# One transformer kernel on Trainium2: the product of w_out and w_gate with w_gate stationary in four column tiles

## The chip, the cores and the metric

The kernel runs on one core of one Trainium2 chip. The metric is the device time of one execution in microseconds, and what is compared is the median of the executions shown. All rows come from one profiled execution of the program. Its engines are TensorE (PE, with its weight loads listed apart as PEld), VectorE (DVE), ScalarE (ACT), GpSimd (POOL) and SyncE (SP), which here only starts transfers.

## What is computed

The reference is attention with a soft cap, followed by a gated product and by a layer of eight experts of which each token uses one:

```python
scores = cap * np.tanh(scale * (q @ k.T) / cap)      # 4 x 12 heads, 448 x 64
attn = softmax(scores); x = attn @ v                 # x: 1792 x 768
x2 = ((x @ w1) * (x @ w2)) @ w3 @ w_out              # 768 -> 1024 -> 1024 -> 768
logits = x2 @ w_gate + modality_bias[modality_id]    # 768 -> 8
e = argmax(logits);  g = softmax(logits)[e]
out = g * (relu(x2 @ moe2_w1[e]) @ moe2_w2[e])
```

The kernel multiplies the weights first: it makes w3 @ w_out once, and it appends to w_out the eight columns of w_out @ w_gate, so that the logits come out of the same products as x2. The product w_out @ w_gate (1024 x 768 by 768 x 8) is what the change touches.

## The kernel before

The first stage, about the first third of the time, does three things interleaved: attention for 24 pairs of heads; the narrowing of the weights, which arrive as 64-bit words and are turned into 32-bit floats by integer operations on VectorE; and the fold, w3 @ w_out, in 32 halves. The order is written by a list planner, `Schedule` (line 20). Each piece of work is a task with an engine (or a choice of two), an estimated duration in ns, a key, the tasks that it depends on, and the buffers that it takes and frees. The planner always emits the task that can start first by its estimates; the engines then run the emitted order, each strictly in its own queue. TensorE tasks also have a mode, "full" for the whole array and "tiles" for 64x64 tiles: the planner charges 190 ns for a change of mode (line 32) and prefers work of the mode that it is in (line 84).

w_out comes in eight chunks of 128 rows. For each chunk c (lines 780 to 815): one load, the narrowing of the chunk into a buffer `y`, two times three transposes by TensorE into a bank of PSUM (`tr_wo`, line 578), each evicted by ScalarE or VectorE (`wo_copy`, line 586) into the tile `woT`; then the gate product (`wo_gate`, line 589), six products that add up over the 768 rows of w_gate; and then `wo_split` (line 594), two VectorE instructions that write the eight columns, as a rounded high part and a low part, beside the chunk's own. The first eight fold pairs need the splits of chunks 0 to 3, the last eight those of chunks 4 to 7. The next chunk's transposes wait for the gate before (`gate[-1:]`, line 797).

The gate, the transposes of k, q, w_out and w3, all take their PSUM bank from one pool of two, "tr" (`bank("tr", 2)`). The 64x64 products of attention (scores line 487, pv line 507, sums line 534) use other banks, `sc` and `pv`.

In the gate before, `lhsT`, the operand that is loaded into the array, is a 128x128 block of w_out transposed, and `rhs`, the one that streams, is 128x8 of w_gate:

```python
for d in range(KD):     # KD = 6
    mm(wo_p[c][:, 0:NE], lhsT=wo_t[c][:, d, :], rhs=wgs[:, d, :], start=(d == 0), stop=(d == KD - 1))
```

The later stages, from about 315 us on, are the large products of the gated layer and of the experts, in an order written in the code; nothing of them is edited.

Of the kernel before, what the change touches and what calls it, by code (L numbers as in the profile page):

```python
# [8 lines left out]
F32 = mybir.dt.float32  # L9
# [5 lines left out]
ALU = mybir.AluOpType  # L15
# [105 lines left out]
def attention_moe_moe_kernel(  # L121
# [37 lines left out]
    nc = tc.nc  # L159
# [3 lines left out]
    NE = w_gate.shape[1]  # L163
    P = 128
    CP = 112
    NC = S // CP
    KD = DM // P
# [32 lines left out]
    at1 = tc.alloc_tile_pool(name="at1", bufs=2, side="right", reuse_waits="tile")  # L200
# [3 lines left out]
    def ctile(name, shape, dt=F32):  # L204
        return cp.tile(shape, dt, name=name, tag=name)

    mm = nc.tensor.matmul
# [3 lines left out]
    ident = ctile("ident", [P, P])  # L211
# [38 lines left out]
    def cast(out_, in_, eng):  # L250
        if eng is nc.scalar:
            nc.scalar.copy(out_, in_)  # L252
        else:
            eng.tensor_copy(out_, in_)
# [8 lines left out]
    class Stream:  # L263
# [17 lines left out]
        def add(self, pieces):  # L281
            n = len(pieces)
            self.todo += [(p, i, n) for i, p in enumerate(pieces)]
# [123 lines left out]
    def bank(tag, bufs):  # L407
        return psa.tile([P, 512], F32, name=tag, tag=tag, bufs=bufs)
# [55 lines left out]
    ENG = {"ACT": nc.scalar, "DVE": nc.vector, "POOL": nc.gpsimd}  # L464
# [71 lines left out]
    def sum_out(p, eng):  # L536
        smt[p] = at1.tile([P, 2, S], F32, name="smt", tag="smt", bufs=2)
        cast(smt[p], smb[p][:, :, :S], ENG[eng])
# [30 lines left out]
    w3raw, w3r = {}, {}  # L569


    wgs = at1.tile([P, KD, NE], F32, name="wgs", tag="wgs", bufs=1)
    wo_y, wo_u, wo_t, wo_p = {}, {}, {}, {}

    def load_wg():
        nc.sync.dma_start(wgs, w_gate.rearrange("(a p) e -> p a e", p=P))

    def tr_wo(c, j):
        if j == 0:
# [6 lines left out]
    def wo_copy(c, j, eng):  # L586
        cast(wo_t[c][:, 3 * j:3 * j + 3, :], wo_p[c, j][:, 0:3 * P].rearrange("p (a f) -> p a f", a=3), ENG[eng])

    def wo_gate(c):
        wo_p[c] = bank("tr", 2)  # L590
        for d in range(KD):
            mm(wo_p[c][:, 0:NE], lhsT=wo_t[c][:, d, :], rhs=wgs[:, d, :], start=(d == 0), stop=(d == KD - 1))

    def wo_split(c):
        g = wo_p[c][:, 0:NE].rearrange("p (a h c) -> p a h c", a=1, h=2)
# [6 lines left out]
    w3p, w3t, fos, sts = {}, {}, {}, {}  # L602
# [126 lines left out]
    def leave_at2():  # L729
# [7 lines left out]
    NW = 14  # L737
    sch = Schedule({
        "raw": 2, "tr": 2, "KT": 3, "QT": 3, "v": NV, "sc": 2, "th": 7, "th3": 2, "sums": 2, "smt": 2, "pv": 1, "pvs": 2,
        "w3raw": 2, "w3r": 2, "w3t": 2, "wst": 2, "wraw": 2, "y": 3, "unit": 5,  # L740
    }, {"SP": 691.0, "ACT": 750.0, "DVE": 1570.0, "POOL": 2010.0, "PE": 1450.0})
    add = sch.add

    def do(fn, *args):
        return lambda: fn(*args)
# [3 lines left out]
    for c in range(30):  # L749
        add("PE", 175, 1e6, lambda: nc.tensor.transpose(warm[:, 0:P], ident, ident),  # L750
            take=[("tr", "warm")] if c == 0 else [], use=[("tr", "warm")])
# [11 lines left out]
    wg_in = add("SP", 630, -4, load_wg, dma=100)  # L763
# [5 lines left out]
    gate, augs = [], []  # L769
# [6 lines left out]
    def cast_c(c, eng):  # L776
        ws.cast1(ENG[eng], False)
        if c < 8:
            wo_u[c] = ws.part
    for c in range(NW):  # L780
        u = c // 2
        key = (4.0 * c + 3) if c < 8 else (10 + 10.0 * c)
        raw, y, un = ("wraw", c), ("y", c), ("unit", u)
        t = add("SP", 630, key - 2, ws.load1, take=[raw], use=[raw], dma=2185, deps=[ld])
        ld = t
        t = add({'ACT': (920, 600), 'DVE': (600, 0)}, 0, key, ws.abs1, [t] + ([ca] if c else []), take=[y], use=[raw, y])
        ca = t
        t = add({'DVE': (630, 0)}, 0, key, lambda eng: ws.narrow1(0, ENG[eng]), [t] + cn3[-1:], use=[raw, y])
        for i in range(1, 4):
            t = add("DVE", 630 if i == 1 else 950, key, do(narrow_c, c, i), [t], use=[raw, y])  # L790
        cn3.append(t)
        if c < 8:
            tt, tp = [("tr", "o", c, j) for j in range(2)], ("tr", "g", c)
            kg = key + 3.0
            cps = []
            for j in range(2):
                x = add("PE", 320, kg, do(tr_wo, c, j), [cn3[-1], *gate[-1:], *cps[-1:]], take=[tt[j], *([] if j else [("th", "o", c)])], use=[tt[j], y, ("th", "o", c)])
                cps.append(add({'ACT': (500, -300), 'DVE': (560, 0)}, 0, kg, lambda eng, c=c, j=j: wo_copy(c, j, eng), [x], use=[tt[j], ("th", "o", c)]))
            gate.append(add("PE", 1500, kg, do(wo_gate, c), [*cps, wg_in], take=[tp], use=[tp, ("th", "o", c)]))
        if c >= 8:  # L800
            kp = add("SP", 650, key - 5, ws.keep1, [t, cs], use=[y], dma=1092)
            t = (kp, 0)
        t = add({'ACT': (730, 0), 'DVE': (470, 600)}, 0, key, lambda eng, c=c: cast_c(c, eng), [t, cs], take=[un] if c % 2 == 0 else [], use=[y, un])

        if c < 8:
            augs.append(add("DVE", 300, key + 3.0, do(wo_split, c), [gate[c], t], use=[tp, un]))

        def sub(eng, c=c):
            ws.sub1(ENG[eng])
            if c % 2 and c < 8:  # L810
                w_outs.append(ws.take())

        cs = units[u] = add({'POOL': (1764, 0)}, 0, key, sub, [t], use=[y, un])
# [7 lines left out]
    for p in range(NP + 1):  # L821
        raw, vk, kt, qt = ("raw", p), ("v", p), ("KT", p), ("QT", p)
        hk, hq, sk, pk = ("tr", "k", p), ("tr", "q", p), ("sums", p), ("pv", p - 1)
        dep, use, take = [], [], []
        if p:
            dep, take, use = [ex[3], lv], [pk], [pk, ("th3", p - 1), ("v", p - 1)]
        if p < NP:
# [4 lines left out]
            t = add("PE", 380, 4 * p - 5.2, do(tr_k, p), [lk], take=[hk], use=[hk, raw])  # L832
            kl = add({'DVE': (620, 0), 'ACT': (530, 300)}, 0, kk, lambda eng, p=p: k_out(p, eng), [t], take=[kt], use=[hk, kt])
            t = add("PE", 380, 4 * p - 5.2, do(tr_q, p), [lq], take=[hq], use=[hq, raw])
            last_at2.append(t)
            ql = add({'DVE': (620, 0), 'ACT': (530, 300)}, 0, kk, lambda eng, p=p: q_out(p, eng), [t], take=[qt], use=[hq, qt])
            dep, take, use = dep + [kl, ql], take + [("sc", p, 3)], use + [("sc", p, 3), kt, qt]
        joint = add("PE", 770, 4 * p, do(pv_score, p), dep, take=take, use=use, mode="tiles")
        if p:

            for c in range(3):
                vl[p - 1, c] = add("PE", 770, 4 * p + c + 2.4, do(pv, p - 1, c), [ex[c], joint, vl.get((p - 1, c - 1))],
                                   use=[pk, ("th", p - 1, c), ("v", p - 1)], mode="tiles")
            smk = ("sc", "s", p - 1)
            sm = add("PE", 770, 4 * p + 2.9, do(sum_mm, p - 1), [ad], take=[smk], use=[smk, ("sums", p - 1)], mode="tiles")
            t = add({'ACT': (910, 0), 'DVE': (1090, 0)}, 0, 4 * p - 1, lambda eng, p=p: sum_out(p - 1, eng), [sm], take=[("smt", p - 1)], use=[smk, ("smt", p - 1)])
            ss = add("SP", 1260, 4 * p, do(sum_store, p - 1), [t], use=[("smt", p - 1)], dma=25)
            t = add("ACT", 530, 4 * p - 2, do(pv_copy, p - 1), [vl[p - 1, 2]], take=[("pvs", p - 1)], use=[pk, ("pvs", p - 1)])
# [4 lines left out]
            if r == H // 2 - 1 and b < B - 1:  # L853
                t = add("SP", 630, 4 * p, lambda b=b: rs_t.__setitem__(b, sums_in(b)), [ss], dma=100)
                t = add("DVE", 500, 4 * p, lambda b=b: sums_add(rs_t[b]), [t])
# [4 lines left out]
        for n, c in enumerate(ORD):  # L860
            sc, th, i = ("sc", p, c), ("th3" if c == 3 else "th", p) + (() if c == 3 else (c,)), 4 * p + n
            if c < 3:
                t = add("PE", 770, i, do(score, p, c), [joint], take=[sc], use=[sc, kt, qt], mode="tiles")
            else:
                t = joint
            t = add("ACT", 600 if c == 3 else 950, i + 0.2, do(p_tanh, p, c), [t, cap_in], take=[th], use=[sc, th])
            ex[c] = add("ACT", 580 if c == 3 else 950, i + 1.1, do(p_exp, p, c), [t], use=[th])
        for c in (1, 2, 3):
            ad = add("DVE", 660 if c == 3 else 1120, 4 * p + 0, do(psum, p, c), [ex[c], *([ex[0]] if c == 1 else []), ad],
                     take=[sk] if c == 1 else [], use=[sk, ("th3", p) if c == 3 else ("th", p, c), *([("th", p, 0)] if c == 1 else [])])  # L870


    t = add("POOL", 1000, 60, tables, [vl[15, 0]])
    t = add("SP", 4000, 60, tables_dma, [t], dma=3000)
# [6 lines left out]
    t = add("SP", 3000, 2 * NH, leave_at2, last_at2, dma=6400)  # L881
# [6 lines left out]
    t = add("SP", 1200, 2 * NH, lambda: raw0[0].append(load_rec(0, 2, xp)), raw0s[:1], dma=1274)  # L888
# [6 lines left out]
    for n, (f, g) in enumerate(SWEEP):  # L895
        key = 5.4 * (n + 2) + 3
        raw, r_, h_, w_ = ("w3raw", n), ("w3r", n), ("tr", "w", n), ("w3t", n)
        t = add("SP", 630, key - 3, do(load_w3, n), take=[raw], use=[raw], dma=1456)
        t = add({'ACT': (660, -300), 'DVE': (610, 0)}, 0, key, lambda eng, n=n: abs_w3(n, eng), [t], take=[r_], use=[raw, r_])
        t = add({'DVE': (500, 0)}, 0, key, lambda eng, n=n: conv_w3(n, 0, eng), [t], use=[raw, r_])  # L900
        for i in range(1, 4):
            t = add("DVE", (0, 425, 690, 910)[i], key, do(conv_w3, n, i), [t], use=[raw, r_])
        t = add("PE", 440, key, do(tr_w3, n), [t], take=[h_], use=[r_, h_])
        t = add({'DVE': (598, 0), 'ACT': (480, 600)}, 0, key - 4, lambda eng, n=n: w3_h(n, eng), [t], take=[w_], use=[h_, w_])
# [3 lines left out]
        for half in range(2):  # L908
# [3 lines left out]
                       take=[] if half else [fo], use=[fo, w_, ("unit", 2 * g), ("unit", 2 * g + 1)])  # L912
# [28 lines left out]
    for i in range(3):  # L941
        t = add("ACT", 840, 0, do(split_x, 0, i, nc.scalar), [out1, raw0s[i]])
        t = add("DVE", 1000, -200, do(split_x, 0, i, nc.vector), [t])
    ld1 = add("SP", 4200, 0, lambda: raws.__setitem__(1, load_raw(1, bp, "xs")), [out1], dma=7650)
    for i in range(3):
        e = nc.vector if i == 1 else nc.gpsimd
        t = add("DVE" if i == 1 else "POOL", 1000 if i == 1 else 2030, 1, do(scale1, i, e), [ld1])
        t = add("ACT", 840, 1, do(split_x, 1, i, nc.scalar), [t])
        t = add("DVE", 1000, 2, do(split_x, 1, i, nc.vector), [t])
# [356 lines left out]
    with tc.For_i(2, nt, 1) as j:  # L1306
        for half in range(2):
            ej = cp.tile([1, 1], I32, name="ej", tag="ej")
            nc.sync.dma_start(ej, evd[half][:, bass.ds(j, 1)])
            e = nc.sync.value_load(ej[0:1, 0:1], min_val=0, max_val=NE - 1)  # L1310
# [3 lines left out]
            t, step = transposer(xs, 0)  # L1314
# [34 lines left out]
```

## Time and profile before

| | us |
|---|---|
| median of 3 executions | 961.33 |
| lowest, highest | 958.78, 965.59 |
| the profiled execution | 963.59 |
| span of the profiled execution (first to last instruction) | 961.7 |
| PE busy in it | 924.1 (96%) |
| DVE busy | 469.1 (49%) |
| ACT busy | 374.9 (39%) |
| POOL busy | 241.0 (25%) |

A row of the profile names an engine, a line of the kernel, an operation, the tiles written and read, the shapes, and how many instructions it stands for (x12). L12 is line 12 of the kernel; where a helper makes the instruction, it is the helper's line (L252 and L254 are the two branches of `cast`). Times in a timeline are counted from the start of the span. An arrow in brackets says how long the engine stood idle before the row and what ended that. A matmul's end is modelled, and it overlaps the next one's start, so start-to-start times say more than its length.

### The profile page before, as it was taken

The numbers are of one execution on the slowest core, as the hardware profiler recorded it, in microseconds if no ns is written. First come the engines' busy times: TensorE is split into PE (matmuls) and PEld (weight loads), VectorE is DVE, ScalarE is ACT, GpSimd is POOL, SyncE is SP. The second block draws the span as 40 slices with busy tenths as digits, with TensorE's granted clock in tenths as the row PEclk, the third lists the DMA queues.
The fourth block names the chain that finished last, engine by engine and source line by source line (L and its number), as shares of the span: only waits on it lengthen the run. The fifth ranks groups of instructions, "written<-read, shape, count | busy, mean of one in ns | idle before, by whom it ended". The sixth has DMA issues, their size and how long they took to land. (4 is left out here: it accounts for less than half of the span.)

```text
span 961.7 us, 13900 instructions
## 1 busy us (share of the span) xinstructions
PE 924.1 (96%) x5618; PEld 763.5 (79%) x5618; DVE 469.1 (49%) x671; ACT 374.9 (39%) x447; POOL 241.0 (25%) x211
## 2 busy tenths in 40 slices
PE   8999989999999999999999999999999999999994
PEld 5456555655655799999999999999899899889894
DVE  4999986786675478721006422100653523423410
ACT  4897766776775333231222211211422312322400
POOL 3434211151110112123542441200604212302011
PEclk9899999999999999999999999999999999999998
DMA  9767785477544565626622341310671591782401
GB/s 225 206 167 219 203 243 141 129 217 179 156 140 121 146 193 164 186 79 215 171 93 96 78 120 34 115 50 33 166 178 43 184 172 33 199 148 52 160 20 44
DMA packets 126088, 132.73 MB, mean 138 GB/s; under 512 B 60926, under 2 KB 107416, under 8 KB 126021
## 3 DMA queue, kind: packets, MB, share of 16 engines
q1 hardware_dynamic: 112644, 114.35, 42.3%
q0 software_dynamic: 12464, 17.22, 7.9%
q8 instruction: 46, 0.75, 0.3%
q10 hardware_dynamic: 912, 0.23, 0.1%
q14 instruction: 22, 0.17, 0.1%
HBM read 102.13 MB, written 30.19 MB: 138 GB/s over the span
## 5 line engine op out<-in xcount | busy, mean ns | idle before, releaser
L1001 PE MATMUL acc<-xT,wh 128*128 128x448 f32 x384 | 141.4, 368 | 0.7 <-DVE xT L935 0.7
L1000 PE MATMUL acc<-xT,wh 128*128 128x448 f32 x384 | 140.4, 366 | 1.5 <-ACT xT L933 1.5
L1002 PE MATMUL acc<-xT,wl 128*128 128x448 f32 x384 | 140.4, 366 | 0.0
L329 DVE TENSOR_TENSOR wl<-raw,wh 128x1536 fp32r<-128x1536 f32 (+1 forms) x42 | 73.6, 1759 | 116.8 <-ACT wh L252 116.8
L252 ACT CAST wh<-raw 128x1536 fp32r<-128x1536 f32 (+1 forms) x48 | 70.3, 1479 | 105.4 <-DMA raw<-in_moe_w_dram 78.5
L487 PE MATMUL sc<-QT,KT 64*64 64x448 f32 x672 | 92.9, 561 | 7.9 <-ACT smt L252 4.2
L507 PE MATMUL pv<-th,vt 64*64 64x448 f32 x672 | 89.2, 551 | 0.0
L498 ACT ACTIVATE th<-th,capb 128x448 f32<-128x448 f32 (+1 forms) x96 | 89.0, 956 | 0.6
L1214 PE MATMUL acc<-wh,hT 128*124 128x384 f32 x256 | 87.8, 343 | 1.1 <-DVE y L1222 0.7
L447 POOL DMA_DIRECT2D vt<-in_v_dram x96 | 50.9, 545 | 146.3 <-PE pv L507 144.9
L1216 PE MATMUL acc<-wh,hT 128*124 128x384 f32 x256 | 86.5, 338 | 0.7 <-DVE hT L1185 0.7
L1215 PE MATMUL acc<-wl,hT 128*124 128x384 f32 x256 | 86.3, 337 | 0.5 <-DVE wl L329 0.5
L1010 POOL TENSOR_TENSOR gT<-a,gT 128x896 fp32r<-128x896 f32 x16 | 43.8, 2740 | 144.2 <-DVE gT L1009 138.7
L1000 PEld LDWEIGHTS acc<-xT,wh 128*128 128x128 f32 x384 | 72.5, 189 | 8.2 <-ACT xT L933 2.3
L1001 PEld LDWEIGHTS acc<-xT,wh 128*128 128x128 f32 x384 | 72.6, 189 | 7.0 <-DVE xT L935 1.2
L492 ACT ACTIVATE th<-sc,icap 128x896 f32<-128x896 f32 x72 | 71.2, 1010 | 16.2 <-PE sc L487 15.6
L1002 PEld LDWEIGHTS acc<-xT,wl 128*128 128x128 f32 x384 | 72.6, 189 | 5.3
L1032 PE MATMUL acc<-wh,gT 128*128 128x388 f32 x224 | 76.4, 341 | 0.0
L1033 PE MATMUL acc<-wl,gT 128*128 128x388 f32 x224 | 76.0, 339 | 0.0
L1034 PE MATMUL acc<-wh,gT 128*128 128x388 f32 x224 | 75.9, 339 | 0.0
L1180 PE MATMUL acc<-xsT,wh 128*128 128x496 f32 x192 | 74.9, 390 | 0.0
L1182 PE MATMUL acc<-xsT,wl 128*128 128x496 f32 x192 | 74.5, 388 | 0.0
(163 smaller groups left out, 1630.1 us busy)
## 6 DMA issues: line engine op xcount, KB each, us to landing
raw<-in_moe_w_dram SPq DMA_DIRECT2D x48, 768.0 KB
w3raw<-in_moe_w_dram SPq DMA_DIRECT2D x16, 512.0 KB
raw<-w_scr SPq DMA_DIRECT2D x8, 776.0 KB
raw<-in_moe_w_out_dram SPq DMA_DIRECT2D x8, 768.0 KB
w_scr<-y SPq DMA_DIRECT2D x16, 384.0 KB
raw<-w_scr SPq DMA_DIRECT2D x8, 768.0 KB
x_scr<-pvs SPq DMA_DIRECT2D x24, 224.0 KB
xraw<-x_scr SPq DMA_DIRECT2D x4, 1344.0 KB
```

Of the source, the lines that this page charges most:

```text
L487: mm(sc[rows_of(side(p, j, g)), g, :S], lhsT=KT[p][rows_of(j), o:o + D], rhs=QT[p][rows_of(j), :], start=True, stop=True)
L498: nc.scalar.activation(tht[p, c], tht[p, c], ACTF.Exp, scale=capb)
L507: mm(pvb[p][rows_of(j), r, :S], lhsT=vt[p][rows_of(r), NC * g + c, :], rhs=tht[p, c][rows_of(r), g, :] if c < NB else tht[p, c][rows_of(r) ...
L1000: mm(acc[:, ft, :S], lhsT=wh[:, o:o + P], rhs=x[:, 0, d, :], start=(d == 0), stop=False)
L1001: mm(acc[:, ft, :S], lhsT=wh[:, o:o + P], rhs=x[:, 1, d, :], start=False, stop=False)
L1002: mm(acc[:, ft, :S], lhsT=wl[:, o:o + P], rhs=x[:, 0, d, :], start=False, stop=(d == KD - 1))
L1032: mm(acc[:, hf, :HA], lhsT=gt[:, 0, f, ts], rhs=wh[:, o:o + HA], start=(f == 0), stop=False)
L1033: mm(acc[:, hf, :HA], lhsT=gt[:, 0, f, ts], rhs=wl[:, o:o + HA], start=False, stop=False)
L1034: mm(acc[:, hf, :HA], lhsT=gt[:, 1, f, ts], rhs=wh[:, o:o + HA], start=False, stop=(f == KF - 1))
L1214: mm(acc[:TP, hf, :HT], lhsT=ht[:, 0, f, cs], rhs=wh[:, o:o + HT], start=(f == 0), stop=False)
L1215: mm(acc[:TP, hf, :HT], lhsT=ht[:, 0, f, cs], rhs=wl[:, o:o + HT], start=False, stop=False)
L1216: mm(acc[:TP, hf, :HT], lhsT=ht[:, 1, f, cs], rhs=wh[:, o:o + HT], start=False, stop=(f == KF - 1))
```

## The change

The operands are swapped. `wgs` gets 32 columns for each of the six blocks of w_gate, 8 real ones and 24 zeros, so that it must be cleared first by GpSimd. A block is loaded into one of four tiles of 128 rows and 32 columns of the array, and the block of w_out transposed streams through it with 128 columns. Products 0 to 3 write 32 partitions of one PSUM bank each; products 4 and 5 add to the first two of these. The four parts then lie below each other, with 8 real rows in each group of 32. `wo_rows` copies them to SBUF on ScalarE or VectorE, and `wo_sum` multiplies them with `pick`, a 128x8 matrix with a one in each row j, j + 32, j + 64 and j + 96 of column j, which adds the four parts and turns the result round as it was before. `pick` is made from the identity by three small VectorE instructions at the start. The planner gets the pieces with new durations (450, 240 or 200, and 250 ns in place of 1500), a third TensorE mode "columns", one more take of a "tr" bank for each chunk, and a pool of two for the copied rows.

```diff
-    wgs = at1.tile([P, KD, NE], F32, name="wgs", tag="wgs", bufs=1)
-    wo_y, wo_u, wo_t, wo_p = {}, {}, {}, {}
+    GC = P // 4
+    wgs = at1.tile([P, KD, GC], F32, name="wgs", tag="wgs", bufs=1)
+    pick = at1.tile([P, NE], F32, name="pick", tag="pick", bufs=1)
+    nc.gpsimd.memset(wgs, 0.0)
+    nc.vector.tensor_tensor(out=pick, in0=ident[:, 0:NE], in1=ident[:, GC:GC + NE], op=ALU.add)
+    for j in range(2, 4):
+        nc.vector.tensor_tensor(out=pick, in0=pick, in1=ident[:, GC * j:GC * j + NE], op=ALU.add)
+    wo_y, wo_u, wo_t, wo_p, wo_g = {}, {}, {}, {}, {}
...
-        nc.sync.dma_start(wgs, w_gate.rearrange("(a p) e -> p a e", p=P))
+        nc.sync.dma_start(wgs[:, :, 0:NE], w_gate.rearrange("(a p) e -> p a e", p=P))
...
     def wo_gate(c):
+        wo_p[c, "t"] = bank("tr", 2)
+        for d in range(KD):
+            j = GC * (d % 4)
+            mm(
+                wo_p[c, "t"][j:j + GC, 0:P], lhsT=wgs[:, d, :], rhs=wo_t[c][:, d, :],
+                start=(d < 4), stop=(d >= KD - 4), tile_position=(0, j), skip_group_check=True,
+            )
+
+    def wo_rows(c, eng):
+        wo_g[c] = at1.tile([P, P], F32, name="wog", tag="wog", bufs=2)
+        cast(wo_g[c], wo_p[c, "t"][:, 0:P], ENG[eng])
+
+    def wo_sum(c):
         wo_p[c] = bank("tr", 2)
-        for d in range(KD):
-            mm(wo_p[c][:, 0:NE], lhsT=wo_t[c][:, d, :], rhs=wgs[:, d, :], start=(d == 0), stop=(d == KD - 1))
+        mm(wo_p[c][:, 0:NE], lhsT=wo_g[c], rhs=pick, start=True, stop=True)
...
-            gate.append(add("PE", 1500, kg, do(wo_gate, c), [*cps, wg_in], take=[tp], use=[tp, ("th", "o", c)]))
+            tq = ("tr", "q", c, "g")
+            x = add("PE", 450, kg, do(wo_gate, c), [*cps, wg_in], take=[tq], use=[tq, ("th", "o", c)], mode="columns")
+            x = add({'ACT': (240, 0), 'DVE': (200, 0)}, 0, kg, lambda eng, c=c: wo_rows(c, eng), [x], take=[("wog", c)], use=[tq, ("wog", c)])
+            gate.append(add("PE", 250, kg, do(wo_sum, c), [x], take=[tp], use=[tp, ("wog", c)]))
```

## Rows read from the trace of the kernel before

**Rows 1.** Busy time by stretch: length, then PE, PEld, DVE, ACT, POOL, PEclk, DMA.

```profile
24.00:48.00 24.00, 22.11 (x178) 10.64 (x181) 22.85 (x34) 21.20 (x30) 10.29 (x11) 0.86 0.71 207
48.00:72.00 24.00, 22.22 (x190) 12.76 (x183) 23.70 (x35) 22.19 (x32) 8.49 (x10) 1.00 0.63 168
...
315.00:940.00 625.00, 621.54 (x3219) 579.96 (x3220) 230.08 (x300) 149.88 (x152) 156.29 (x81) 1.00 0.44 120
```

**Rows 2.** Timeline of PE, 34 to 38 us: start, length, instruction.

```profile
34.09 0.92 PE L487 MATMUL sc<-QT,KT 64*64 64x448 f32 x8
...
37.10 0.92 PE L507 MATMUL pv<-th,vt 64*64 64x448 f32 x8
37.95 0.55 PE L584 MATMUL tr<-ident,y 128*128 128x128 f32 x3
```

**Rows 3.** Timeline of PE around the third gate.

```profile
52.42 0.55 PE L584 MATMUL tr<-ident,y 128*128 128x128 f32 x3
52.90 0.59 PE L487 MATMUL sc<-QT,KT 64*64 64x448 f32 x2
...
53.81 1.50 PE L592 MATMUL tr<-wgs,woT 128*128 128x8 f32 x12
55.17 0.58 PE L474 MATMUL tr<-ident,q 112*128 112x112 f32 x4
```

**Rows 4.** PE by line, 48 to 72 us: count, busy us, mean ns, idle before.

```profile
L487 PE MATMUL sc<-QT,KT 64*64 64x448 f32 x52 | 7.1, 552 | 0.0
L507 PE MATMUL pv<-th,vt 64*64 64x448 f32 x48 | 6.4, 540 | 0.0
L592 PE MATMUL tr<-wgs,woT 128*128 128x8 f32 x24 | 3.0, 258 | 0.0
...
L534 PE MATMUL sc<-sums,sel 64*64 64x448 f32 x16 | 1.9, 547 | 0.0
...
L649 PE MATMUL sc<-wl,w3h 128*128 128x388 f32 x5 | 1.7, 340 | 0.0
```

**Rows 5.** Evictions and splits by line: ns min/median/max, first and last start.

```profile
L252 ACT COPY woT<-tr x13: 473/482/537, 26.2 to 103.7; 128x384 f32<-128x384 f32 x13
L254 DVE COPY woT<-tr x3: 546/549/551, 23.9 to 114.5; 128x384 f32<-128x384 f32 x3
...
L597 DVE CAST wh<-tr x8: 148/151/161, 30.0 to 123.0; 128x8 fp32r<-128x8 f32 x8
```

**Rows 6.** Timeline of PE: the first two gates, with the idle time before.

```profile
28.30 1.48 PE L592 MATMUL tr<-wgs,woT 128*128 128x8 f32 x12 [1.23 <-DVE KT L254]
...
41.46 1.50 PE L592 MATMUL tr<-wgs,woT 128*128 128x8 f32 x12 [0.66 <-ACT woT L252]
```

**Rows 7.** Busy time by stretch again: three stretches after gates, PEclk third from last.

```profile
29.80:33.20 3.40, 3.40 (x20) 1.35 (x23) 3.37 (x7) 2.44 (x4) 0.00 (x0) 0.50 0.48 106
...
43.50:46.90 3.40, 3.40 (x20) 1.18 (x24) 3.37 (x6) 2.35 (x5) 2.41 (x1) 0.50 0.64 209
...
53.80:57.20 3.40, 3.40 (x36) 2.40 (x36) 3.37 (x6) 3.40 (x6) 2.19 (x1) 1.00 0.77 264
```

**Rows 8.** Timeline of all engines at the start.

```profile
1.17 0.14 POOL L413 MEMSET sel<- 128x64 f32 x1
...
3.26 0.43 SPq L576 DMA_DIRECT2D wgs<-in_moe_w_gate_dram x1
...
7.93 0.16 DVE L757 RECIPROCAL icap<-capb 128x1 f32<-128x1 f32 x1 [6.18 <-DMA capb<-in_cap_dram]
```

**Rows 9.** Timelines of PE and DVE after the fourth gate.

```profile
65.85 0.58 PE L474 MATMUL tr<-ident,q 112*128 112x112 f32 x4
...
68.65 0.63 PE L619 MATMUL tr<-ident,w3r 128*128 128x128 f32 x4 [1.30 <-DVE wl L598]
...
68.15 0.15 DVE L597 CAST wh<-tr 128x8 fp32r<-128x8 f32 x1
```

**Rows 10.** Timeline of PE: the first product of the next stage.

```profile
315.21 0.47 PE L1000 MATMUL acc<-xT,wh 128*128 128x448 f32 x1 [1.48 <-ACT xT L933]
```

More of the change, by code (lines that the diff above doesn't have):

```diff
@@ L739, in attention_moe_moe_kernel @@
         "raw": 2, "tr": 2, "KT": 3, "QT": 3, "v": NV, "sc": 2, "th": 7, "th3": 2, "sums": 2, "smt": 2, "pv": 1, "pvs": 2,
-        "w3raw": 2, "w3r": 2, "w3t": 2, "wst": 2, "wraw": 2, "y": 3, "unit": 5,
+        "w3raw": 2, "w3r": 2, "w3t": 2, "wst": 2, "wraw": 2, "y": 3, "unit": 5, "wog": 2,
     }, {"SP": 691.0, "ACT": 750.0, "DVE": 1570.0, "POOL": 2010.0, "PE": 1450.0})
```

## The prediction

> **What bounds the kernel now.** The page's busy times come first: TensorE is the fullest engine. But the change touches only the first third of the span, so I read busy time by stretch next. There the reader is to see two regimes. From 315 us on TensorE fills its time and the vector and scalar engines are idle for more than half of it; nothing of that stage is edited. Eight gates run in the first stage, two in each 24 us. In the first two such stretches VectorE is busy 22.85 and 23.70 of 24 us and ScalarE 21.20 and 22.19, with TensorE's record at 22.11 and 22.22 [rows 1]. TensorE's figure is flattering, because a record goes on after the next has started. So I read the start-to-start times. Thirty-two records of 64x64 products, four array tiles at a time, take 34.09 to 37.10, or 0.094 us each [rows 2]. The gate starts twelve records in 53.81 to 55.17, 0.113 us each [rows 3]; a transpose loads 128 columns as they do, so I give it the same. In the stretch 48 to 72 us that makes 116 records x 0.094 = 10.9, 24 gate records x 0.113 = 2.7, and 50 others: 35 transposes at 0.113 (4.0) and 15 fold products (three lines like L649, five each) at no more than their own record of 0.34 (5.1); together at most 22.7 of 24 us [rows 4]. So TensorE has some slack there, the two evicting engines have hardly any, and what is taken off TensorE is worth between nothing and its full size. I take half.
>
> **What it removes.** Six products of a chunk, each two records (a gate's row counts twelve [rows 3]), with 128 columns to load and 8 to stream. One chunk is 1.36 us, the eight 10.9 us.
>
> **What it adds on TensorE.** Again six products and twelve records, but with 128 columns streaming through tiles of 32 columns. No row shows that shape. The nearest is the 64x64 mode: a slot of four records with 448 columns takes 4 x 0.094 = 0.375 us, so 128 columns take 0.107 us. If four column tiles run at once as these four do, products 0 to 3 take two slots (two records each) and products 4 and 5 two more: 4 x 0.107 = 0.43 us. If they run one after another it is 12 x 0.107 = 1.28 us. I take 0.43, because the 64x64 rows show four tiles starting together, at a pitch a quarter of a slot; but in those rows two tiles share each half of the rows, and here four would. A change of mode: the last two slots of 37.10 end at 37.85, and the transposes start at 37.95, so 0.10 us [rows 2]; the way back is 52.42 to 52.90 less three transposes at 0.113, 0.14 us [rows 3]. I take 0.12. A gate that stands between tiles and transposes has one change more than before; a sum that lands alone among 64x64 work has two. I take two more per chunk, 0.24, with bounds of one (0.12) and three (0.36). The sum is one full product, two records at 0.113, 0.22 us. A chunk is then 0.43 + 0.24 + 0.22 = 0.89 us, 0.47 less than before; for eight 3.8 us less. The bounds: 0.43 + 0.12 + 0.22 = 0.77, 4.7 us less; and 1.28 + 0.36 + 0.22 = 1.86, 4.0 us more. At half its worth the value taken is -1.9 us.
>
> The Trainium skill, TensorEngine Tiling (Array Packing), Performance Considerations, says that where the streamed operand is at most 32 wide one should swap the operands and tile the columns fourfold. By its factor of up to four, an estimate from that page, a chunk would cost 0.34 us and the eight save 8.2 us; no run here has shown this mode yet. The sum above doesn't use it.
>
> **What it adds on ScalarE or VectorE.** Eight evictions of 128x128. Shown are 128x384 in 0.482 us (ScalarE) and 0.549 us (VectorE), and 128x8 in 0.151 us (VectorE) [rows 5]; those bound it, and on a line between the two VectorE rows it is 0.28 us. Eight are 2.2 us. In 48 to 72 us the two engines have 0.3 and 1.8 us free [rows 1], and two evictions want 0.56 of it. Shared by two engines this is 1.1 us on each, and at half its worth +0.5 us; the bounds are 0 and 8 x 0.55 = 4.4. Behind a late eviction stand the sum, then the two split instructions of the vector engine and the fold products that need the split.
>
> **The handoffs.** Before, the gate went to the split; now there is an eviction and a product between. TensorE waited ahead of the gates only at the first two, 1.23 us for a copy of keys and 0.66 for an eviction of w_out's transposes [rows 6]. Eight sums, which wait for one eviction each, would by the luck of the eight gates stand 0.7 us in all. I add +0.7 (bounds 0 and 1.9, both waits met again). Queued behind a waiting sum are transposes and scores, and for these wait the copies and the tanh on ScalarE.
>
> **The clock.** Granted is 2.4 GHz nearly everywhere. Two dips to 1.2 GHz, 29.8 to 33.2 and 43.5 to 46.9 us, each begin within a microsecond after a gate, before which TensorE had stood 1.2 and 0.7 us; after the gate at 53.8 us, which had no wait before it, there is none [rows 3, 6, 7]. In a dip TensorE does half, so each costs up to 1.7 us of its work. A gate that is short and streams 128 columns could save one; I count one of two at half its worth, -0.9 us (bounds 0 and -3.4).
>
> **Start, and what costs nothing.** The GpSimd memset of 128x192 is at most three times the 128x64 one, 0.44 us; it precedes the loads of v on GpSimd's queue and the load of w_gate on SP's, which starts at 3.26 us, when the memset (from 1.3 us on) is long done [rows 8]. If that cover were gone it would cost the 0.44 us. The three tiny vector instructions (0.15 us each by the 128x8 row) lie in VectorE's idle 6.18 us that ends at 7.93 [rows 8]; without that cover, 0.5 us. The load of w_gate has as many 32-byte pieces as before.
>
> **The sum.** -1.9 + 0.5 + 0.7 - 0.9 = -1.6 us. Against the profiled execution, 963.59 (its span is 961.7, and the 1.9 us around it stay), that is 962.0. The profiled execution stands 2.3 us over the median of the three, 961.33, so at the median I forecast 959.7, rounded to 960.
>
> **The rivals.**
> *It goes slower: the two small banks.* The gate, the sum, and all transposes of k, q, w_out and w3 rotate through two PSUM banks "tr". At chunk 3 the gate was done by 65.85, but VectorE came to its split at 68.15, and TensorE stood 1.30 us before the transposes of w3, released by the split [rows 9]. Now each chunk takes a bank twice, and the second time only after an eviction. If TensorE stands 1.30 us more at each chunk, that is 8 x 1.30 = 10.4, and the shorter gate buys nothing: 971.7 us. It decides once the next instruction in TensorE's order needs a bank while the split is over 1 us late, at all chunks and not at one or two. For it speaks the load of VectorE and ScalarE; against it, that scores and pv products need no such bank and the order written out by the planner can put them between. The Trainium skill, TensorEngine Tiling, PSUM Bottleneck, warns of just this side: after tiling, the PSUM copy may bind. Chance 0.08.
> *It goes faster: TensorE decides in full.* The switches fall at borders that are paid anyway, a chunk costs 0.43 + 0.22, 8 x 0.71 = 5.7 us saved in full, both dips go (3.4) and so do the waits ahead of the two early gates (1.9): -11.0, 950.3 us. For it: TensorE is the fullest engine over the span. Against: VectorE has 0.3 us free in 48 to 72 us, so it would have to follow. The swap rule of the Trainium skill's TensorEngine Tiling would lead here too if its factor of four held. Chance 0.08.
> *It doesn't do what it says: the column tiles run one after another.* Then TensorE has 4.0 us more, half of it +2.0, with +0.5 and +0.7 and no dip saved: +3.2, 964.5 us. For it: no row shows four tiles over the same 128 rows. Against: the 64x64 rows. Chance 0.16.
> *The forecast,* about 960 us: chance 0.68; its own range goes from all 3.8 us saved with both dips (-7.2, 954 us) to nothing saved with every eviction at its upper bound (+4.4, 966 us).
>
> **How the numbers follow.** About 1% (9.6 us) is what a measurement of this kernel can tell from no change. The forecast and the serial rival lie inside it: 0.68 + 0.16 = 0.84. The fast and slow rivals lie just outside, 0.08 each. The range takes in the forecast's own range and the serial rival with the three times' spread (958.78 to 965.59) around it, and leaves out the two outer rivals: 953 to 968 us.
>
> **What would show it.** In the profile after: right if the twelve gate records span about 0.4 us with starts in fours, and wrong (the serial rival) if over 1.2 us; the switch, if the record after the last gate record starts 0.1 to 0.2 us late; the eviction, if the 128x128 copies last near 0.28 us; the handoff and the banks, in TensorE's idle time before the sums and before transposes, released by the eviction or by the split; the dips, in the granted clock between 28 and 50 us; the whole, in the start of the first product of the next stage, 315.21 us before [rows 10]. Most of all the planner orders everything anew with other durations: if that start moves by more than 4 us without any of these rows moving, the order itself did it, which no row of before prices.

## The result, and the profile after

The changed kernel takes 957.6 us (median of 11 executions, 953.17 to 960.05) against 965.42 for the kernel before beside it (11 executions, 958.78 to 970.22). The ratio is 0.9916, with a 95% interval of 0.9892 to 0.9939. That is 0.84% faster. The forecast was 960 in 953 to 968 and "within 1%", and both hold, but the gain is four to five times the 1.6 us of the sum. Over the executions beside the experiments the mean is 963.9 us for before (103, on four chips), and over all executions of the changed kernel it is 957.2 us (32), 6.7 us apart; this is the number to explain. One execution of the kernel old_product below, 978.78 us against 963.47 for its fastest, was a slow one and is left out of its ratio, mean and clock.

The gate itself came out as forecast. Timeline of TensorE around the third gate of the changed kernel (start, length, instruction):

```profile
57.24 0.63 PE L600 MATMUL tr<-woT,wgs 128*32 128x128 f32 x12
57.80 0.98 PE L507 MATMUL pv<-th,vt 64*64 64x448 f32 x8
...
59.46 0.39 PE L611 MATMUL tr<-pick,wog 128*128 128x8 f32 x2
59.70 0.73 PE L460 MATMUL tr<-ident,k 128*128 128x128 f32 x4
```

The reader is to see that the twelve records and the change of mode behind them end after 0.56 us (57.24 to 57.80), and that the sum takes 0.24 (59.46 to 59.70) and runs two groups of attention later. Together 0.80, where before it was 1.36 [rows 3]. The Trainium skill, TensorEngine Tiling (Array Packing), Performance Considerations, names a fourfold column tiling for such a swap; a quarter of the old time would be 0.34 us, an estimate from that page. Here the gate with its change of mode takes 0.41 of the old time and with the sum 0.59, so the measurement lies above that.

Eviction of the parts, by line (ns min/median/max, first and last start):

```profile
L254 DVE COPY wog<-tr x4: 275/284/292, 29.4 to 113.5; 128x128 f32<-128x128 f32 x4
L252 ACT COPY wog<-tr x4: 268/272/285, 68.7 to 130.4; 128x128 f32<-128x128 f32 x4
```

These are the 0.28 us that the line through [rows 5] gave, four on each engine. TensorE's waits between 20 and 135 us (total us, times, longest):

```profile
PE tr L591 <- ACT woT L252: 3.4, 2, 2.9
PE tr L474 <- DVE KT L254: 3.1, 2, 2.0
...
PE tr L591 <- DVE wl L617: 0.7, 1, 0.7
```

One wait of 0.7 us is left for the split (L617 now), so the rival of the two banks [rows 9] didn't come. Waits for other copies grew: all waits of this kind come to 10.7 us here and came to 5.8 before in the same window, so part of the time that the gates gave back TensorE spent waiting. Busy time by stretch (length, then PE, PEld, DVE, ACT, POOL, PEclk), to be laid beside [rows 1]:

```profile
24.00:48.00 24.00, 19.64 (x165) 8.64 (x161) 20.39 (x32) 18.93 (x26) 6.43 (x10) 0.86 0.68 173
48.00:72.00 24.00, 22.38 (x204) 9.82 (x197) 23.15 (x34) 22.18 (x34) 11.55 (x11) 1.00 0.63 187
```

The second stretch holds 204 records where there were 190, with the vector and scalar engines as full as before, but the first holds 165 where there were 178, so over the two TensorE is no further. Nor is it by 135 us, behind the last gate. From there to the next stage, first the changed kernel, then before:

```profile
135.00:312.83 177.83, 169.52 (x1398) 99.53 (x1396) 128.48 (x197) 128.06 (x165) 38.36 (x67) 1.00 0.62 172
135.00:315.21 180.21, 169.03 (x1372) 102.48 (x1369) 122.70 (x189) 127.17 (x164) 35.79 (x67) 0.99 0.57 162
```

TensorE still has 169.5 us of work, against 169.0, and the lead in this profile comes only after that, where it stands idle for 8.3 us instead of 11.2. The first product of the next stage:

```profile
312.83 0.47 PE L1022 MATMUL acc<-xT,wh 128*128 128x448 f32 x1 [1.48 <-ACT xT L955]
```

It starts 2.4 us earlier than in [rows 10]. This one profiled execution took 960.05 us, the longest of its eleven and 3.5 us under the profiled execution of before, so this pair of profiles shows half of the 6.7 us. The dips of the clock tell why one profile is not enough. First the changed kernel's, then two of before that [rows 7] don't have:

```profile
29.20:32.60 3.40, 3.40 (x19) 1.06 (x15) 3.40 (x6) 1.31 (x2) 0.00 (x0) 0.50 0.65 156
42.90:46.30 3.40, 3.40 (x27) 1.37 (x28) 3.10 (x6) 1.21 (x3) 0.00 (x0) 0.50 0.67 120
90.60:94.00 3.40, 3.04 (x15) 1.30 (x19) 0.38 (x1) 1.89 (x4) 1.80 (x1) 0.51 0.98 350
...
145.90:149.30 3.40, 3.40 (x24) 2.02 (x20) 2.52 (x6) 1.96 (x3) 0.00 (x0) 0.50 0.00 1
316.50:320.00 3.50, 3.50 (x10) 3.11 (x11) 1.78 (x2) 0.33 (x1) 0.00 (x0) 0.51 0.95 295
```

Both early dips of [rows 7] are still there in this profile, and each kernel has a third one in the first stage, at 90.6 and at 145.9 us. Before has a fourth behind the start of the next stage, which the change does not touch. But every execution records its mean granted clock, and over all of them that is 0.9903 for the changed kernel and 0.9873 for before. In a dip half of 3.4 us is lost, 0.0018 of the span, so the difference of 0.0030 is between one and two dips fewer per execution. That mean is over the whole span: it also counts dips of the later stage, and in every profile a stretch at half clock at the end (the last 6.9 us before, the last 7.5 in the changed kernel), in which TensorE has no work.

### The profile page after: what moved, and what is told of

It is laid out like the page before. It is cut to its first block, busy times and chain, and to the rows that moved or that the text cites. A ratio compares the mean times of both kernels' runs of the same rounds, so it can differ in the third digit from the quotient of the medians.

```text
span 958.3 us, 13933 instructions
## 1 busy us (share of the span) xinstructions
PE 916.9 (96%) x5634; PEld 752.7 (79%) x5634; DVE 470.6 (49%) x676; ACT 377.9 (39%) x453; POOL 240.1 (25%) x212
## 5 line engine op out<-in xcount | busy, mean ns | idle before, releaser
L492 ACT ACTIVATE th<-sc,icap 128x896 f32<-128x896 f32 x72 | 71.4, 1007 | 11.9 <-PE sc L487 11.2
```

## The experiments

I began with three theories. A, the prediction's: TensorE's time counts by half. B: the planner's new order made the gain. C: TensorE's time counts in full. A fourth, D, came after the first four runs: the clock pays a part. Every ratio is to the kernel before on the same chip. "Clock" is the mean granted clock over the executions.

| kernel | median us | ratio, 95% interval | clock |
|---|---|---|---|
| before (four chips) | 963.1 to 964.3 | | 0.987 |
| after_again | 957.43 | 0.9928, 0.9899 to 0.9956 | 0.991 |
| after_third | 956.47 | 0.9932, 0.9907 to 0.9957 | 0.990 |
| one_tile | 962.52 | 0.9973, 0.9951 to 0.9995 | 0.991 |
| old_product | 967.91 | 1.0032, 1.0003 to 1.0061 | 0.985 |
| old_plan | 955.74 | 0.9915, 0.9881 to 0.9949 | 0.992 |
| old_plan_again | 956.40 | 0.9926, 0.9897 to 0.9954 | 0.991 |
| measured | 956.97 | 0.9932, 0.9906 to 0.9958 | 0.992 |
| new_price | 961.78 | 0.9979, 0.9954 to 1.0004 | 0.987 |
| padded | 961.86 | 0.9989, 0.9964 to 1.0014 | 0.991 |
| rows_thrice | 962.23 | 0.9978, 0.9952 to 1.0003 | 0.989 |
| rows_off | 958.42 | 0.9949, 0.9923 to 0.9976 | 0.990 |
| gate_thrice | 963.51 | 1.0000, 0.9974 to 1.0026 | 0.991 |

**The changed kernel again, twice.**

> The changed kernel, unaltered, beside the others on their chip. All theories: the ratio to before again between 0.989 and 0.994, so some 8 us faster. The first product of the next stage starts near 312.8 us in the profile, as in the first profile of it (315.2 before); if it starts elsewhere by more than 1 us, the first stage varies from execution to execution by itself.

> The changed kernel once more, as the neighbour of the other three on their chip: 957 to 958 us, 0.7 to 0.8% under before, clock 0.990 to 0.991.

The gain is there on two more chips, 0.7%. The next stage starts at 311.2 us in the one profile and at 309.5 in the other, not at 312.8: the first stage varies by itself, as the first expectation allowed. Of the dips after the first two gates each of these profiles has one (at 45.1 and at 39.3 us), and one more near 88 us.

**Is it the order? Two kernels that change the plan alone (new_price and measured), and one, run twice, with the new products under the old price.**

```diff
# new_price, in the kernel before
-            gate.append(add("PE", 1500, kg, do(wo_gate, c), ...
+            gate.append(add("PE", 700, kg, do(wo_gate, c), ...
# old_plan (run twice), in the changed kernel
-            x = add("PE", 450, kg, do(wo_gate, c), ..., mode="columns")
-            x = add({'ACT': (240, 0), 'DVE': (200, 0)}, ...
-            gate.append(add("PE", 250, kg, do(wo_sum, c), ...
+            x = add("PE", 1500, kg, do(wo_gate, c), ...)
+            x = add({'ACT': (1, 0), 'DVE': (1, 0)}, ...
+            gate.append(add("PE", 1, kg, do(wo_sum, c), ...
# measured, in the changed kernel: 465, (272, 284) and 240 in the same places
```

> The kernel before with one number changed: the planner charges 700 ns for the old gate in place of 1500. Only the order of the work changes. Theory B (order): 3 us or more faster than before. Theories C and D: within 2 us of before, with a clock near 0.987.

> The new products under the old price: the planner is told 1500 ns, whole-array mode, for the gate and 1 ns for the eviction and the sum, so the work around it stands as close to the order of before as the added tasks allow. Theory A and C (TensorE's time): most of the gain stays, within 3 us of the changed kernel. Theory B (the order): the gain goes, within 2 us of the kernel before.

> The new products under the old price, a second time, next to the changed kernel. If the order that the new price gives is worth nothing or less: 0 to 2.5 us faster than the changed kernel. If the first result was luck: within 1 us of it or slower.

> The changed kernel with the planner's durations set to what the profile shows: 465 ns for the gate, 272 and 284 for the eviction, 240 for the sum, in place of 450, 240, 200 and 250. Another order of nearly the same price, so what differs is the order's luck alone: within 2 us of the changed kernel by every theory; more would mean that the order alone moves as much as the products do.

The new products under the old price keep the whole gain in both runs (0.9915 and 0.9926), and a plan with true durations gives the same time again (0.9932). The old product under a lower price gains 0.2% with an interval that reaches past 1. So theory B is out as the main cause: under the old product the new price is worth 1.9 us in the mean, uncertain by 2 either way, and under the new products the order is worth less than can be told.

**What is TensorE's time worth? All six products in one column tile, and the gate made three times.**

```diff
# one_tile
-            j = GC * (d % 4)
-                wo_p[c, "t"][j:j + GC, 0:P], ..., start=(d < 4), stop=(d >= KD - 4), tile_position=(0, j), ...
+                wo_p[c, "t"][0:GC, 0:P], ..., start=(d == 0), stop=(d == KD - 1), tile_position=(0, 0), ...
# the eviction then copies 32 rows, and the sum has lhsT=wo_g[c][0:GC, :], rhs=ident[0:GC, 0:NE]
# gate_thrice
-        for d in range(KD):
+        for d in [*range(KD)] * 3:
```

> The changed kernel with all six products in the first column tile, one after another, and the sum over these 32 rows alone; the planner's durations, and so the order of the work, are untouched. The gate's twelve records take 12 x 0.108 = 1.3 us instead of 0.47, 6.6 us more for eight. Theory A (TensorE's time counts by half): 3.3 us slower than the changed kernel. Theory B (the new order made the gain, whatever the product takes): within 1.5 us of the changed kernel. Theory C (TensorE's time counts in full): 6.6 us slower, the gain all but gone.

> The changed kernel with each gate's twelve records made three times over, the last time counting: 8 x 2 x 0.43 = 6.9 us more on TensorE, nothing more on the other engines, streams of 128 columns as before, the planner not told. The mean granted clock should stay near 0.990. TensorE's time at full worth: 6.9 us slower than the changed kernel, 964 us or as slow as before. At the 0.65 that the single column tile showed: 4.5 us. At the prediction's half: 3.4 us.

Timeline of TensorE around the third gate, first with one tile:

```profile
54.77 1.50 PE L599 MATMUL tr<-woT,wgs 128*32 128x128 f32 x12
56.20 0.98 PE L507 MATMUL pv<-th,vt 64*64 64x448 f32 x8
...
57.86 0.38 PE L610 MATMUL tr<-ident,wog 32*128 32x8 f32 x2
58.18 0.75 PE L460 MATMUL tr<-ident,k 128*128 128x128 f32 x4
```

And with the gate made three times:

```profile
55.38 1.50 PE L600 MATMUL tr<-woT,wgs 128*32 128x128 f32 x36
56.82 0.98 PE L507 MATMUL pv<-th,vt 64*64 64x448 f32 x8
```

In one tile the twelve records take 1.43 us with the change of mode (54.77 to 56.20), and thirty-six records in four tiles take 1.44: the tiles do run side by side, threefold here, since products 4 and 5 fill only two of the four tiles. Against 0.56 both are 0.87 to 0.88 us more per chunk, 7.0 for eight. The one-tile kernel also pays 0.08 us more for its sum (57.86 to 58.18), 7.6 in all. Its mean is 962.4, 5.1 us over the changed kernel's 957.2, and the thrice-made gate's is 963.9, 6.7 over. TensorE's time counts by 0.7 (0.5 to 0.9 with two standard errors) and by 0.96 (0.7 to 1.2). The single tile alone would just allow theory A's half, the gate made three times does not: the half is too low, and C is nearer. The granted clock is the changed kernel's in both.

**The old product in the new order.**

```diff
-            mm(wo_p[c, "t"][j:j + GC, 0:P], lhsT=wgs[:, d, :], rhs=wo_t[c][:, d, :], ...
+            mm(wo_p[c, "t"][:, 0:NE], lhsT=wo_t[c][:, d, :], rhs=wgs[:, d, :], start=(d == 0), stop=(d == KD - 1))
# evicted are 128x8, and the sum's place holds a product with the identity
```

> The order of the changed kernel with the product of before in it: six products with 128 columns loaded and 8 streamed (1.36 us against 0.47 and a change of mode of 0.1 to 0.2), an eviction of 128x8 in place of 128x128, and in the sum's place a product with the identity that only passes the columns on. TensorE has 8 x 0.75 = 6 us more. Theory A: 3 us slower than the changed kernel. Theory B: within 1.5 us of it. Theory C: 6 us slower.

It is slower than every theory said: 968.3 us in the mean, 5.9 over the one-tile kernel on the same chip, though the records stand for about the same time:

```profile
62.39 1.50 PE L598 MATMUL tr<-wgs,woT 128*128 128x8 f32 x12
63.83 0.98 PE L507 MATMUL pv<-th,vt 64*64 64x448 f32 x8
...
65.49 0.39 PE L606 MATMUL tr<-wog,ident 128*128 128x8 f32 x2
65.74 0.73 PE L460 MATMUL tr<-ident,k 128*128 128x128 f32 x4
```

That is 1.44 and 0.25 us, against 1.43 and 0.32 with one tile. What differs is the clock, 0.985 against 0.991 over the executions. Its profile shows four dips before the next stage, three of them longer than any above (length first, the granted clock third from last):

```profile
27.90:38.10 10.20, 10.20 (x53) 4.92 (x56) 7.53 (x13) 4.87 (x8) 0.00 (x0) 0.50 0.39 95
45.00:51.80 6.80, 6.21 (x32) 4.18 (x32) 4.86 (x8) 2.40 (x4) 0.00 (x0) 0.50 0.17 39
96.20:103.00 6.80, 5.76 (x31) 2.29 (x35) 3.27 (x7) 4.82 (x8) 1.80 (x1) 0.50 0.76 253
202.00:205.40 3.40, 3.40 (x24) 1.20 (x20) 3.40 (x8) 2.30 (x3) 1.12 (x1) 0.50 0.63 205
```

Together they are 27.2 us at half clock, where the one-tile kernel's profile has 6.8 before the next stage. Half of the difference is 10.2 us, and the next stage starts 9.9 us later (324.4 against 314.55): in these two profiles the clock is enough for all of it. Over the executions the clock's 0.0062 is three to four dips of 1.7 us, 5.9 us by that count, as much as the two kernels are apart. From this run on, theory D.

**The old product, padded.**

```diff
# in the kernel before
-    wgs = at1.tile([P, KD, NE], F32, ...)
+    wgs = at1.tile([P, KD, 96], F32, ...); nc.gpsimd.memset(wgs, 0.0)
-            mm(wo_p[c][:, 0:NE], lhsT=wo_t[c][:, d, :], ...
+            mm(wo_p[c][:, 0:96], lhsT=wo_t[c][:, d, :], ...
```

> The kernel before with w_gate's blocks padded with zeros to 96 columns: each of the old products loads 128 columns as before and streams 96 in place of 8. The planner, the order and the number of instructions are those of before; TensorE's records stay at 0.11 us apart, since the load sets that. Theory D (a gate that streams few columns lets the clock fall, and each dip costs 1.7 us): the mean granted clock over the executions rises from 0.987 to about 0.991 and the kernel is 3 us faster than before. Theory C (TensorE's time alone): clock and time as before, within 1 us.

The clock rose as D said, from 0.9869 (29 executions) to 0.9909 (12), with the order of before and the same number of records. The time did not follow as far: 962.0 against 963.4 in the mean, 1.4 us less with an interval that reaches past 1, where 3 was expected. A part is the records' pitch:

```profile
50.87 1.58 PE L594 MATMUL tr<-wgs,woT 128*128 128x96 f32 x12
52.28 0.55 PE L474 MATMUL tr<-ident,q 112*128 112x112 f32 x4
```

Twelve take 1.41 us instead of 1.36, 0.4 us for eight. So padding alone moved the granted clock; that the clock gives back its full price in time is not shown by this run. With the 0.4 us added back it is 1.8 us for 0.0040, or 0.45 us for each 0.001 of clock, uncertain by about as much.

The profiles point the same way, though each is one draw. Between the first gate and the next stage, the three kernels with 8 columns streamed stand at half clock for 10.2 us (before), 10.2 (new_price) and 27.2 (old_product), the padded one for 6.8, and the ten profiles with 128 columns for 3.4 to 10.2, 6.5 in the mean.

**What is an eviction worth? Made three times, or followed by two copies that nobody waits for.**

```diff
# rows_thrice: the eviction stands in a loop
+        for _ in range(3):
             cast(wo_g[c], wo_p[c, "t"][:, 0:P], ENG[eng])
# rows_off: behind one eviction, on the same engine
+        for i in range(2):
+            cast(other, ident, ENG[eng])
```

> The changed kernel with each eviction of the four parts made three times in place of once, on the same engine, 8 x 2 x 0.28 = 4.5 us more on the vector and scalar engines and 0.56 us more from each gate to its sum; the planner isn't told. The prediction's half worth: 1.1 us slower than the changed kernel. If these two engines set the stage: 4.5 us. If they have slack and only TensorE counts: within 1 us.

> The changed kernel with two more 128x128 copies behind each eviction, on the same engine, from one constant tile in SBUF to a scratch tile that nothing reads: the engines' time as with the thrice-made eviction (about 4.5 us more), but the sum waits no longer and the bank is freed as early. If the engines' time was what the thrice-made eviction paid for (4 to 5 us): again 4 us slower than the changed kernel. If it paid for the longer way from the gate to the sum: within 1.5 us of the changed kernel.

Two copies off the way cost 1.9 us (958.8 against 956.9 in the mean, with a standard error of 1.2) for 8 of 0.215 us on VectorE and 8 of 0.303 on ScalarE, 4.1 us. That is near the prediction's half, but anything from nothing to the full size fits. On the way, the same number of copies, 4.5 us, costs 4.8 us against the changed kernel's mean on other chips. That the difference of 2.9 us is what the longer way from the gate to the sum costs is not shown; its standard error is about 1.5. Weight loads of TensorE for which the eviction was the last to come, 20 to 135 us, in the thrice-evicting kernel:

```profile
PEld tr L612 <- ACT wog L252: 2.2, 3, 0.8
...
PEld tr L612 <- DVE wog L254: 0.7, 1, 0.7
```

With one eviction there is 0.7 us of such waits. But this is not more waiting: all idle time of the weight loads before the eight sums, whatever ended it, is 5.8 us with one eviction and 5.0 with three, and TensorE's products themselves, in the view shown above for the changed kernel, wait for an eviction of the parts in neither. Nor are the copies off the way quite off it, since they come last before two sums (1.4 us).

## Why the prediction was right, and where it was not

**TensorE's saving.** Forecast 0.89 us a chunk, measured 0.56 + 0.24 = 0.80: 4.5 us saved instead of 3.8. The gate's slots, the change of mode, the sum and the side-by-side tiles held. (Away from dips and waits, the 0.56 is the same at every gate.) The serial rival is out by the rows, and the one-tile kernel shows what it would have been.

**The half.** This is the term that was too small. I read slack out of busy shares: at most 22.7 of 24 us of work on TensorE [rows 1, 4], so a microsecond there was to be worth between nothing and one. The two kernels that add TensorE time put it at 0.7 and 0.96. The stage's order is written in advance and each engine takes it in its queue, so an instruction that comes later pushes what stands behind it, whether or not the engine has idle time elsewhere. That reason is argued; the two worths are measured, on time added and not on time taken away. At these worths the saving is 3.1 to 4.3 us instead of 1.9.

**The clock.** The mechanism was named, its size was not. I took one of two dips, at half its worth: -0.9. The mean clock went up by 0.0030. Across the 103 executions of before, 0.001 of clock goes with 0.80 us, so this would be 2.4 us; but that is a correlation, and the padded kernel, which moved little but the clock, gave 0.45 us for 0.001, which would be 1.3. The place was half right: of the two early dips the first profile of the changed kernel keeps both, the other two keep one. No single profile could have settled the count.

**The evictions and handoffs.** Length exact (0.28). Their worth is open: by the copies off the way 0.46, with an error as large as the half, by the thrice-made eviction about 1. At 0.46 it is +1.0 for 2.2 us, where I had +0.5 since I had divided it between the engines. The waits of sums for evictions are 0.7 us in the profile after, the number forecast, but on the weight loads; TensorE's products did not stand for it.

**The sum again,** with what was measured: -3.1 to -4.3, -1.3 to -2.4, +1.0 and +0.7, that is -2.7 to -5.0, against 6.7 measured. Some 2 to 4 us are not placed. They may lie in the order (the old product under the lower price had 1.9 us less, with an interval that reaches past no change), or in the price of the clock, which these runs give only within a factor of two. The profiles don't place them, since between the gates TensorE's waits grew from 5.8 us to 8.5 to 10.7 in the three of the changed kernel. This stays open.

**The number.** That 960 came within 2.4 us of 957.6 is in part luck. The sum was taken from the median of three executions, 961.33, and the mean of 103 is 963.9; from there it would have been 962.3, 4.7 us too slow. The base was too low by 2.6 us, the gain too small by 5.1, and the first hid half of the second.

**The rivals.** The slow one (banks) did not show in any row. The fast one (TensorE in full, both dips) was the nearer to the mechanism, but at -11.0 it took savings that did not come: dips stayed, and the early gates' waits went to their neighbours (in its three profiles 0.6 to 2.0 us stand before the transposes of q behind the first gate, and 2.1 before those of w3 ahead of the second).

## What to carry to other kernels

In a stage whose order is written out ahead, price a microsecond added on the engine that carries most of it at more than half, up to its full size, even when busy shares show slack. What work on the engines that feed it is worth, these runs don't settle: 1.9 us for 4.1 off the way, with a wide error, and 4.8 for 4.5 on it. Swap a thin product's operands so that the wide one streams: here the tiles of columns ran at once, and the granted clock of the kernel rose with it. Where the clock falls and recovers within a stage, read its mean over many executions, because one profile has one draw of the dips, and look in the profile for stretches at half clock in which the engine has no work, since they count in that mean and cost nothing.

## What the runs showed of the hardware

Four tiles of 128 rows and 32 columns take float32 products at the same time: twelve records in 0.56 us against 1.43 in one tile, change of mode included. The same twelve weight loads of 128 columns with 96 columns streamed instead of 8 take 1.41 us instead of 1.36, and the kernel's mean granted clock goes from 0.987 to 0.991; with the 8-column product in the changed kernel's order it was 0.985. The Trainium skill, TensorE: Matmul & The Clock Gate, Part 1, tells that the clock is set by how busy TensorE has been; these runs agree that it moves with what TensorE does, and add that two kernels with the same order and nearly the same record times can be granted different clocks.
